# Whole float32 W1out and g in the first half batch, shifts shared with VectorE, and quarters of W1 in alternating order by batch

## The chip, the core and the metric

One of the eight cores of a Trainium2 chip runs the kernel. The metric is device time in microseconds (us) of one execution; lower is better. Engines are named as in the profile: PE (TensorE) with PEld (its weight loads), DVE (VectorE), ACT (ScalarE), POOL (GpSimd), SP (SyncE, which issues most DMAs).

## What is computed

Four batches of 8 heads, 576 tokens and 64 channels go through a Nystrom attention with 32 landmarks; the tokens (2304 x 512) then pass two MLPs with 2048 hidden channels:

```
q_lm, k_lm = q, k averaged over 18 tokens each
A = softmax(q k_lm' / 8); Bm = softmax(q_lm k_lm' / 8); C = softmax(q_lm k' / 8)
Z = 6 Newton steps towards the inverse of Bm
x = A Z C v
h = x @ w_in;  x = (h - tanh(h)) @ w_out                    # first MLP
h = x @ w_in2; out = (h * tanh(softplus(h))) @ w_out2       # second MLP
```

The weights arrive as 64-bit floats and are turned into 32-bit ones on the chip.

## The kernel before

**Order of the work.** The first MLP is a pipeline of 128 slots: four batches of 32, each batch two halves of 288 tokens, each half 16 blocks f of 128 hidden channels. The attention's last product is folded into W1in: P = Z0 times W1in for a batch (`p_gen`, a quarter j of 512 hidden channels at a time, two groups g of heads), and h of a slot is P times the attention weights AT (`h1`, six fp32r matmuls, L511 to L513, on two groups). `vec` then makes g from h on ACT and DVE: a square, a tanh, an exp and another square on ACT; a mask mk, two operations on h, a product and a masked copy on DVE. Two slots later `vec` splits g into a high and a low fp32r half (gg; ACT copies, DVE or POOL subtracts, L99 and L100), and three slots later (LAG = 3) `y1` multiplies it with block f of W1out, split in the same way (w). Each product takes three fp32r matmuls, high by high (L614), low weights by high (L615) and high weights by low g (L618), for four quarters d of the output: 12 a slot. After 16 slots y goes to DRAM (ys). The second MLP follows, in slots of 384 tokens (`h2`, `o2`).

**Weights.** `convert` takes a list of jobs, each a 512 KB load of 64-bit floats into one of four raw buffers (L115). `f32_a` makes the upper part on ACT (L131) and the lower part by a shift, on ACT (L137) or on DVE (L140); `f32_b` merges them on DVE (L144). The list's argument `act_share` says which jobs shift on ACT: all at 1, every second one at 2. A `keep_job` leaves half of a W1in tile (w1) and writes the finished tile to DRAM (w1s, a spill, L171, issued from POOL) for the later batches, which load it back for each `p_gen` (L477). A `split_job` splits a W1out block into w at once (L99, L100). 13 jobs come before the first slot (quarter 0 of W1in, W1out blocks 0 to 8), three more follow, and the rest run beside slots 0 to 11.

**What sets the order.** Up to slot 115 a scheduler orders each engine's instructions by priority and dependencies; from slot 116 they stand as written. Each engine takes its own in order. The helper `E()` gives DVE up to slot 23 and after slot 103, POOL between. The attention of the next batch runs beside slots 5 to 31 of a batch.

## Time and profile before

| | us |
|---|---|
| median of 3 runs (lowest, highest) | 851.7 (851.68, 852.64) |
| the profiled execution's own time | 851.59 |
| its span | 849.8 |
| PE busy | 812.7 (96%) |
| DVE busy | 503.3 (59%) |
| ACT busy | 496.6 (58%) |
| POOL busy | 179.0 (21%) |

The profiled execution takes 1.8 us more than its span, since the span counts from the first instruction to the last. Times below are from the span's start. Busy shares are means over stages with different limits, so they have to be read stage by stage.

### The profile page before, as it was taken

Reading aid. Unit: us, or ns where it says so; the run is one execution under the profiler, and the core shown is the slowest. Engines: PE = TensorE matmul, PEld = TensorE weight load, DVE = VectorE, ACT = ScalarE, POOL = GpSimd, SP = SyncE. Lnnn points to the kernel's source line nnn. Section 1 sums busy time; section 2 is a strip of 40 time slices with the busy share of each in tenths; the row PEclk is TensorE's granted clock in tenths of the full one; section 3 lists DMA queues with packets and bytes.
Section 4 is the critical chain, followed back from the end, with each engine's and each line's share of the span. In section 5 each row is a group of like instructions: output and inputs, shape, how many; then the busy total and the mean of one; then the engine's idle time right before and its main releaser. Section 6 shows DMA issues by size and latency. Waiting matters only on the chain.

```text
span 849.8 us, 15003 instructions
## 1 busy us (share of the span) xinstructions
PE 812.7 (96%) x5656; PEld 706.5 (83%) x5656; DVE 503.3 (59%) x1158; ACT 496.6 (58%) x1234; POOL 179.0 (21%) x210
## 2 busy tenths in 40 slices
PE   4599899999999999999999999999999999999998
PEld 1346689889988899879899999999999999999996
DVE  6878999998789877999973986322111111211111
ACT  5888976788778886799874865333223222222221
POOL 0010003886577666870000000000000000000000
PEclk9557999999999999999999999999999999999999
DMA  9899240430415100360006662022002001000000
GB/s 327 289 338 366 105 136 6 148 136 1 141 51 183 51 30 1 119 215 20 29 2 225 202 195 69 1 66 74 1 1 66 10 1 49 18 1 9 30 1 37
DMA packets 34985, 79.62 MB, mean 94 GB/s; under 512 B 5472, under 2 KB 14176, under 8 KB 34912
## 3 DMA queue, kind: packets, MB, share of 16 engines
q1 hardware_dynamic: 33760, 74.46, 26.0%
q0 software_dynamic: 1152, 4.19, 1.2%
q8 instruction: 44, 0.72, 0.4%
q14 instruction: 29, 0.24, 0.1%
HBM read 65.01 MB, written 13.63 MB: 93 GB/s over the span
## 4 chain that ended last, share of the span: by engine, by line
PE 74%; DVE 12%; ACT 5%; POOL 3%; DMA 2%; issue 2%; SPq 0%; DVEq 0%; ACTq 0%
PE y L642 7%; PE y L638 7%; PE y L637 7%; PE y L614 6%; PE h L537 5%; PE h L536 5%; PE h L535 5%; PE y L618 5%; PE y L615 5%; PE m L211 3%; PE m L537 2%; PE h L511 2%; PE m L536 2%; PE m L535 2%; DVE g L596 2%; PE h L513 2%
## 5 line engine op out<-in xcount | busy, mean ns | idle before, releaser
L585 DVE TENSOR_TENSOR gg<-g,gg 128x384 fp32r<-128x384 f32 x96 | 53.5, 558 | 276.0 <-ACT g L584 276.0
L614 PE MATMUL y<-gg,w 128*128 128x288 f32 x512 | 151.3, 310 | 5.4 <-ACT gg L99 4.1
L615 PE MATMUL y<-gg,w 128*128 128x288 f32 x512 | 143.8, 296 | 0.0
L614 PEld LDWEIGHTS y<-gg,w 128*128 128x128 f32 x512 | 97.0, 189 | 29.4 <-issue 15.3
L618 PE MATMUL y<-gg,w 128*128 128x288 f32 x512 | 109.8, 299 | 1.2 <-DVE gg L100 0.8
L583 ACT ACTIVATE gg<-h 128x384 fp32r<-128x384 f32 x66 | 32.5, 492 | 132.8 <-PE h L537 132.8
L638 PE MATMUL y<-w,gg 128*128 128x512 f32 x256 | 101.2, 395 | 0.0
L637 PE MATMUL y<-w,gg 128*128 128x512 f32 x256 | 100.8, 394 | 0.0
L615 PEld LDWEIGHTS y<-gg,w 128*128 128x128 f32 x512 | 97.5, 190 | 0.0
L100 POOL TENSOR_TENSOR gg<-g,gg 128x288 fp32r<-128x288 f32 x80 | 69.3, 866 | 115.8 <-ACT gg L99 113.8
L642 PE MATMUL y<-w,gg 128*128 128x512 f32 x256 | 88.4, 396 | 0.0
L618 PEld LDWEIGHTS y<-gg,w 128*128 128x128 f32 x512 | 81.7, 189 | 6.3 <-DVE gg L100 2.1
L511 PE MATMUL h<-AT,P 128*128 128x288 f32 x256 | 79.0, 309 | 8.2 <-ACT P L490 5.1
L568 POOL TENSOR_SCALAR mk<-s 128x288 uint8<-128x288 f32 x80 | 77.7, 972 | 10.5 <-ACT s L562 4.3
L513 PE MATMUL h<-AT,P 128*128 128x288 f32 x256 | 77.7, 303 | 0.2 <-DVE P L492 0.2
L512 PE MATMUL h<-AT,P 128*128 128x288 f32 x256 | 77.8, 304 | 0.0
L596 DVE COPY_PREDICATED g<-mk,th 128x288 f32<-128x288 uint8 x128 | 74.3, 580 | 4.6
L99 ACT ACTIVATE gg<-g 128x288 fp32r<-128x288 f32 x128 | 57.1, 446 | 24.3 <-PE y L618 15.4
L578 ACT ACTIVATE q<-q,bias_c 128x288 f32<-128x288 f32 x128 | 69.1, 540 | 2.2
L574 DVE TENSOR_TENSOR g<-h,s 128x288 f32<-128x288 f32 x128 | 56.9, 445 | 19.5 <-ACT th L563 18.9
L583 ACT ACTIVATE gg<-m 128x384 fp32r<-128x384 f32 x30 | 14.8, 492 | 89.2 <-PE m L537 89.2
L562 ACT ACTIVATE s<-h 128x288 f32<-128x288 f32 x128 | 52.6, 411 | 23.9 <-PE h L513 23.8
(162 smaller groups left out, 1856.9 us busy)
## 6 DMA issues: line engine op xcount, KB each, us to landing
w<-w1s SPq DMA_DIRECT2D x24, 512.0 KB, 4.5
raw<-in_w1i_dram SPq DMA_DIRECT2D x16, 512.0 KB, 6.5
raw<-in_w1o_dram SPq DMA_DIRECT2D x16, 512.0 KB, 4.8
raw<-in_w2i_dram SPq DMA_DIRECT2D x16, 512.0 KB, 4.5
raw<-in_w2o_dram SPq DMA_DIRECT2D x16, 512.0 KB, 4.2
ys<-raw SPq DMA_DIRECT2D x16, 288.0 KB, 2.4
out_dram<-raw SPq DMA_DIRECT2D x18, 256.0 KB, 2.2
v<-in_v_dram SPq DMA_DIRECT2D x8, 512.0 KB, 8.5
```

Of the source, the lines that this page charges most:

```text
L100: eng.tensor_tensor(out=L, in0=src, in1=f32(H), op=ALU.subtract)
L511: mm(p, P[:, g, 0, c], AT[:, g, 0, :], start=(g == 0), stop=False)
L512: mm(p, P[:, g, 0, c], AT[:, g, 1, :], start=False, stop=False)
L513: mm(p, P[:, g, 1, c], AT[:, g, 0, :], start=False, stop=(g == NG - 1))
L568: eng.tensor_scalar(out=mk, in0=e, scalar1=FT, scalar2=None, op0=ALU.is_ge)
L596: V.copy_predicated(out=g0, mask=mk0, data=t0)
L614: mm(yps[d], w[:, 0, c], gg[:, 0, :], start=(f == 0), stop=False)
L615: mm(yps[d], w[:, 1, c], gg[:, 0, :], start=False, stop=False)
L618: mm(yps[d], w[:, 0, c], gg[:, 1, :], start=False, stop=(f == NF - 1))
L637: mm(p, gg[:, 0, cs], w[:, 0, :], start=(f == 0), stop=False)
L638: mm(p, gg[:, 0, cs], w[:, 1, :], start=False, stop=False)
L642: mm(p, gg[:, 1, cs], w[:, 0, :], start=False, stop=(f == NF - 1))
```

## The change

In the first half batch (slots 0 to 15, `NW`), y1 multiplies whole float32 g with whole float32 W1out: one matmul for each d (L646 in the changed program), which the chip runs as two instructions. W1out blocks are kept whole by `whole_job` and split by `resplit`, one block a slot in slots 14 to 29. `convert` shifts every second job on DVE. `hidden` lets odd batches take the quarters of W1 in the order 3, 2, 1, 0 (but for the last half batch), so that two quarters of a batch stay in SBUF for the next and only two are loaded back. The prologue converts quarters 0 and 1 and five W1out blocks. Spills of quarters 2 and 3 are written later in the program, at slot 14. The splits of P get a high priority.

```diff
-    NPRE = 9
+    NPRE = 5
+    NW = 16
...
-    wo_p = ctx.enter_context(tc.tile_pool(name="wo", bufs=NF))
+    wo_p = ctx.enter_context(tc.tile_pool(name="wo", bufs=NF + 1))
...
+    def spill(g, j):
+        G.dma_start(out=w1s[g, j], in_=w1t[g, j])
+
+    def whole_job(src, dst, i):
+        def where():
+            W1f[i] = wo_p.tile([128, 2, 512], F32, tag="w", name="w")
+            return W1f[i][:, 0, :]
...
+    def resplit(i):
+        w = wo_p.tile([128, 2, 512], F32R, tag="w", name="w")
+        A.activation(out=w[:, 0, :], in_=W1f[i][:, 0, :], func=ACTF.Copy)
+        yield 1
+        E().tensor_tensor(out=w[:, 1, :], in0=W1f[i][:, 0, :], in1=f32(w[:, 0, :]), op=ALU.subtract)
+        W1o[i] = w
+        yield 1
...
             if a == 1:
-                G.dma_start(out=w1s[g, j], in_=w1t[0, g, j])
+                if j < 2:
+                    spill(g, j)
...
+    def hidden(s):
+        b, hf, p = s // 32, s // 16 % 2, s % 16
+        return 4 * (3 - p // 4) + p % 4 if b % 2 and not (b == B - 1 and hf) else p
...
-        n = 2 * (4 * b + j) + 2
-        if b or j == 3:
-            w1_load(n)
-            w1_load(n + 1)
+        if b and n == 1:
+            w1_load(js[2])
+            w1_load(js[3])
...
-            A.activation(out=P[:, g, 0, :], in_=p, func=ACTF.Copy)
+            with tc.high_priority(60):
+                A.activation(out=P[:, g, 0, :], in_=p, func=ACTF.Copy)
...
-        if 2 <= s < NS + 2:
+        if 2 <= s < NW + 2:
+            sv[s - 2] = sv[s - 2][0]
+        if NW + 2 <= s < NS + 2:
...
-                gg = tp[1].tile([128, 2, C2], F32R, tag="gg", name="gg", bufs=5)
+                gg = tp[1].tile([128, 2, C2], F32R, tag="gg", name="gg", bufs=4)
...
-        w = W1o[f]
-        for d in (2 * half, 2 * half + 1):
+        w = W1o[hidden(s)]
+        for d in (2 * half, 2 * half + 1) if s < NW else ():
+            if f == 0:
+                yps[d] = ps_y.tile([128, 512], F32, tag="y", name="y")[:, 0:HS]
+            mm(yps[d], w[:, 0, 128 * d:128 * d + 128], gg, start=(f == 0), stop=(f == NF - 1))
+        for d in (2 * half, 2 * half + 1) if s >= NW else ():
...
-            return [split_job(src[i], wo_p, "w", dst, i) for i in range(lo, hi)]
+            return [whole_job(src[i], dst, i) for i in range(lo, hi)]
-        jobs = w1i_jobs(0) + wo_jobs(w1o, W1o, 0, NPRE)
-        rest = [(4 * j, n) for j in (1, 2, 3) for n in w1i_jobs(j)]
+        jobs = w1i_jobs(0) + w1i_jobs(1) + wo_jobs(w1o, W1o, 0, NPRE)
+        rest = [(4 * j - 2, n) for j in (2, 3) for n in w1i_jobs(j)]
...
-        cv = vec_only(convert(jobs), rate)
+        cv = vec_only(convert(jobs, 2), rate)
...
+                if i == 14:
+                    for j in (2, 3):
+                        for g in range(NG):
+                            spill(g, j)
+                if NW - 2 <= i < NW - 2 + NF:
+                    streams.append(resplit(i - NW + 2))
```

On PE, the work of one slot's y1. Before (y_695, y_698, y_717 and y_720 are the four quarters d, w_266 a W1out block):

```order
L614 MATMUL y_695<-gg_791,w_266 128x288
L615 MATMUL y_695<-gg_791,w_266 128x288
L614 MATMUL y_698<-gg_791,w_266 128x288
L615 MATMUL y_698<-gg_791,w_266 128x288
L614 MATMUL y_717<-gg_791,w_266 128x288
L615 MATMUL y_717<-gg_791,w_266 128x288
L618 MATMUL y_695<-gg_791,w_266 128x288
L618 MATMUL y_698<-gg_791,w_266 128x288
L614 MATMUL y_720<-gg_791,w_266 128x288
L615 MATMUL y_720<-gg_791,w_266 128x288
L618 MATMUL y_717<-gg_791,w_266 128x288
L618 MATMUL y_720<-gg_791,w_266 128x288
```

and of the change, with the first h matmul behind it:

```order
L646 MATMUL y_687<-g_754,w_505 128x288
L646 MATMUL y_689<-g_754,w_505 128x288
L646 MATMUL y_705<-g_754,w_505 128x288
L646 MATMUL y_707<-g_754,w_505 128x288
L542 MATMUL h_863<-AT_484,P_578 128x288
```

The twelve fp32r matmuls have become four on g itself.

On DVE, one slot in the middle of the first half batch. Before (raw, y: a weight's lower and upper part; w: a W1out block; red: landmark sums of batch 1):

```order
L100 TENSOR_TENSOR gg_950<-g_849,gg_950 128x288
L144 SCALAR_TENSOR_TENSOR y_902<-y_902,raw_753 128x512
L568 TENSOR_SCALAR mk_957<-s_953 128x288
L100 TENSOR_TENSOR w_970<-y_857,w_970 128x512
L574 TENSOR_TENSOR g_955<-h_916,s_953 128x288
L575 TENSOR_TENSOR th_954<-h_916,th_954 128x288
L592 TENSOR_TENSOR g_955<-q_956,g_955 128x288
L250 TENSOR_REDUCE red_837<-k_708 128x64
L596 COPY_PREDICATED g_955<-mk_957,th_954 128x288
```

and of the change:

```order
L141 TENSOR_SCALAR raw_768<-raw_768 128x512
L145 SCALAR_TENSOR_TENSOR w_887<-y_849,raw_733 128x512
L601 TENSOR_SCALAR mk_878<-s_874 128x288
L607 TENSOR_TENSOR g_876<-h_863,s_874 128x288
L608 TENSOR_TENSOR th_875<-h_863,th_875 128x288
L625 TENSOR_TENSOR g_876<-q_877,g_876 128x288
L275 TENSOR_REDUCE red_797<-k_696 128x64
L629 COPY_PREDICATED g_876<-mk_878,th_875 128x288
```

The subtractions for gg and w are gone from the slot, and a shift (L141) has come in.

On POOL, from the last spill on; its first g split is that of slot 22, in slot 24. Before (c: attention of batch 1; xm: its row statistics):

```order
L171 DMA w1s_78<-w1_807 128x1024
L100 TENSOR_TENSOR gg_1828<-g_1745,gg_1828 128x288
L568 TENSOR_SCALAR mk_1835<-s_1831 128x288
L100 TENSOR_TENSOR gg_1875<-g_1792,gg_1875 128x288
L568 TENSOR_SCALAR mk_1882<-s_1878 128x288
L100 TENSOR_TENSOR gg_1915<-g_1833,gg_1915 128x288
L445 TENSOR_TENSOR c_1087<-c_1087,xm_1893 128x288
L568 TENSOR_SCALAR mk_1922<-s_1918 128x288
L445 TENSOR_TENSOR c_1087<-c_1087,xm_1934 128x288
L100 TENSOR_TENSOR gg_1956<-g_1880,gg_1956 128x288
```

and of the change:

```order
L165 DMA w1s_78<-w1_722 128x1024
L101 TENSOR_TENSOR gg_1648<-g_1559,gg_1648 128x288
L601 TENSOR_SCALAR mk_1655<-s_1651 128x288
L183 TENSOR_TENSOR w_1637<-w_887,w_1637 128x512
L101 TENSOR_TENSOR gg_1698<-g_1609,gg_1698 128x288
L601 TENSOR_SCALAR mk_1705<-s_1701 128x288
L183 TENSOR_TENSOR w_1680<-w_921,w_1680 128x512
L183 TENSOR_TENSOR w_1733<-w_956,w_1733 128x512
L101 TENSOR_TENSOR gg_1741<-g_1653,gg_1741 128x288
L601 TENSOR_SCALAR mk_1748<-s_1744 128x288
L183 TENSOR_TENSOR w_1777<-w_999,w_1777 128x512
L470 TENSOR_TENSOR c_972<-c_972,xm_1717 128x288
```

Six W1out subtractions (L183, two more come further on) now stand between the g splits and masks, ahead of batch 1's attention. In both programs the spills follow each other at the front of POOL's queue with nothing between them.

## Rows read from the trace of the kernel before

**Rows 1.** Stages: window, length, busy PE, PEld, DVE, ACT, POOL, clock, DMA, GB/s.

```profile
0.00:45.00 45.00, 24.63 (x285) 11.53 (x286) 33.45 (x85) 32.98 (x73) 2.00 (x8) 0.70 0.89 309
45.00:83.00 38.00, 36.42 (x169) 21.14 (x170) 33.09 (x79) 30.59 (x73) 3.30 (x6) 0.68 0.96 353
83.00:114.00 31.00, 25.75 (x185) 20.75 (x184) 29.95 (x77) 27.56 (x75) 0.00 (x0) 1.00 0.26 96
114.00:139.00 25.00, 25.00 (x336) 22.50 (x335) 23.68 (x71) 18.96 (x53) 0.00 (x0) 1.00 0.36 120
139.00:163.00 24.00, 23.54 (x199) 20.11 (x198) 21.24 (x47) 18.75 (x50) 19.12 (x22) 1.00 0.15 50
```

**Rows 2.** The chain that ended last: start us, us, what; from 84.21 DVE throughout.

```profile
50.76 8.44 DMA raw<-in_w1i_dram
...
84.21 0.69 DVE w L100
...
106.93 0.38 DVE th L575
```

**Rows 3.** PE's timeline (start us, us): last h of slots 0, 8, 16, 24.

```profile
45.14 0.44 PE L513 MATMUL h<-AT,P 128*128 128x288 f32 x1
...
83.40 0.30 PE L513 MATMUL h<-AT,P 128*128 128x288 f32 x1
...
113.67 0.30 PE L512 MATMUL h<-AT,P 128*128 128x288 f32 x1
113.81 0.30 PE L513 MATMUL h<-AT,P 128*128 128x288 f32 x1
...
139.01 0.30 PE L513 MATMUL h<-AT,P 128*128 128x288 f32 x1
```

**Rows 4.** PE's timeline: a burst of fp32 matmuls and the next fp32r one.

```profile
333.56 0.72 PE L211 MATMUL m<-q,kb 64*32 64x288 f32 x16
334.20 0.40 PE L614 MATMUL y<-gg,w 128*128 128x288 f32 x1
```

**Rows 5.** Groups by line, 0 to 114 us: count, busy us, mean ns, idle before.

```profile
L144 DVE SCALAR_TENSOR_TENSOR y<-y,raw 128x512 uint32<-128x512 uint32 x16 | 10.9, 682 | 1.7 <-ACT raw L137 1.4
L100 DVE TENSOR_TENSOR w<-y,w 128x512 fp32r<-128x512 f32 x16 | 10.9, 682 | 0.8 <-ACT w L99 0.8
L100 DVE TENSOR_TENSOR gg<-g,gg 128x288 fp32r<-128x288 f32 x14 | 6.2, 443 | 0.6 <-ACT gg L99 0.6
...
L137 ACT ACTIVATE raw<-raw 128x512 uint32<-128x512 uint16 x32 | 21.5, 670 | 0.0
```

**Rows 6.** The shift on DVE, in the second MLP (min/median/max ns).

```profile
L140 DVE TENSOR_SCALAR raw<-raw x13: 419/421/426, 458.4 to 533.6; 128x512 uint32<-128x512 uint32 x13
```

**Rows 7.** The page's DMA issues: W1 tiles loaded back.

```profile
w<-w1s SPq DMA_DIRECT2D x24, 512.0 KB, 4.5
```

**Rows 8.** Timelines of PE and ACT: P of quarter 0, and its first copy.

```profile
34.63 1.96 PE L211 MATMUL m<-w,z 64*32 64x512 f32 x16 [0.93 <-ACT z L415]
...
39.70 0.57 ACT L490 ACTIVATE P<-m 128x512 fp32r<-128x512 f32 x1
```

**Rows 9.** Timelines: POOL's g splits of slots 22 and 29; PE's use of the latter.

```profile
139.08 0.81 POOL L100 TENSOR_TENSOR gg<-g,gg 128x288 fp32r<-128x288 f32 x1 [63.54 <-ACT gg L99]
...
160.60 0.89 POOL L100 TENSOR_TENSOR gg<-g,gg 128x288 fp32r<-128x288 f32 x1
...
161.99 0.43 PE L618 MATMUL y<-gg,w 128*128 128x288 f32 x2
```

**Rows 10.** POOL's groups by line, 139 to 163 us.

```profile
L568 POOL TENSOR_SCALAR mk<-s 128x288 uint8<-128x288 f32 x8 | 7.7, 962 | 0.7
L100 POOL TENSOR_TENSOR gg<-g,gg 128x288 fp32r<-128x288 f32 x8 | 6.9, 866 | 66.7 <-ACT gg L99 66.6
L100 POOL TENSOR_TENSOR AT<-c,AT 128x288 fp32r<-128x288 f32 x2 | 1.6, 808 | 0.3 <-ACT AT L99 0.3
L457 POOL TENSOR_TENSOR c<-c,xm 128x288 f32<-128x288 f32 x2 | 1.5, 760 | 0.2
```

More of the change, by code (lines that the diff above doesn't have):

```diff
@@ L161, in split_job, with done @@
         return src, done, None
+    def spill(g, j):
[4 more added lines that the diff above has]
+            return W1f[i][:, 0, :]
+        def done(y):
+            dst[i] = W1f[i]
+        return src, done, where
+    W1f = {}
+    def resplit(i):
[5 more added lines that the diff above has]
+        yield 1
     def keep_job(src, g, j, a):
@@ L165, in where @@
             if a == 0:
-                w1t[0, g, j] = w1_p.tile([128, 2, 512], F32, tag="w1", name="w1")
-            return w1t[0, g, j][:, a, :]
+                w1t[g, j] = w1_p.tile([128, 2, 512], F32, tag="w1", name="w1")
+            return w1t[g, j][:, a, :]
         def done(y):
             if a == 1:
-                G.dma_start(out=w1s[g, j], in_=w1t[0, g, j])
+                if j < 2:
+                    spill(g, j)
                 if g:
@@ L470, with w1_load, p_gen @@
     done = set()
-    def w1_load(n):
-        b, j, g = n // 8, n // 2 % 4, n % 2
-        if b < B:
-            t = w1_p.tile([128, 2, 512], F32, tag="w1", name="w1")
-            w1t[b, g, j] = t
-            nc.sync.dma_start(out=t, in_=w1s[g, j])
-    def p_gen(b, j):
-        ws = [w1t.pop((b, g, j)) for g in range(NG)]
+    def hidden(s):
+        b, hf, p = s // 32, s // 16 % 2, s % 16
+        return 4 * (3 - p // 4) + p % 4 if b % 2 and not (b == B - 1 and hf) else p
+    def w1_load(j):
+        for g in range(NG):
+            w1t[g, j] = w1_p.tile([128, 2, 512], F32, tag="w1", name="w1")
+            nc.sync.dma_start(out=w1t[g, j], in_=w1s[g, j])
+    def p_gen(b, n):
+        js = [hidden(32 * b + 4 * i) // 4 for i in range(4)]
+        j = js[n]
         P = Pt[b, j] = P_p.tile([128, NG, 2, 512], F32R, tag="P", name="P")
         pp = [ps_m.tile([128, 512], F32, tag="m", name="m") for g in range(NG)]
-        blocks(pp, Z0, lambda ps, g, a: ws[g][ps, a, :])
-        n = 2 * (4 * b + j) + 2
-        if b or j == 3:
-            w1_load(n)
-            w1_load(n + 1)
+        blocks(pp, Z0, lambda ps, g, a: w1t[g, j][ps, a, :])
+        if b and n == 1:
+            w1_load(js[2])
+            w1_load(js[3])
         yield 1
         for g, p in enumerate(pp):
-            A.activation(out=P[:, g, 0, :], in_=p, func=ACTF.Copy)
+            with tc.high_priority(60):
+                A.activation(out=P[:, g, 0, :], in_=p, func=ACTF.Copy)
             yield 0
-            V.tensor_tensor(out=P[:, g, 1, :], in0=p, in1=f32(P[:, g, 0, :]), op=ALU.subtract)
+            with tc.high_priority(60):
+                V.tensor_tensor(out=P[:, g, 1, :], in0=p, in1=f32(P[:, g, 0, :]), op=ALU.subtract)
             yield 0
@@ L504, in h1 @@
     def h1(s):
-        b, hf, f = s // 32, s // 16 % 2, s % 16
+        b, hf, f = s // 32, s // 16 % 2, hidden(s)
         AT, P = ATt[b, hf], Pt[b, f // 4]
@@ L615, in y1 @@
             mm(yps[d], w[:, 1, c], gg[:, 0, :], start=False, stop=False)
-        for d in (2 * half, 2 * half + 1):
+        for d in (2 * half, 2 * half + 1) if s >= NW else ():
             c = slice(128 * d, 128 * d + 128)
@@ L779 @@
                     del live[k]
-            if "pre" not in live and ready and nc_ >= 4 + NPRE - 1:
+            if "pre" not in live and not Pt and nc_ >= 8 + NPRE - 1:
                 pg = p_gen(0, ready.pop(0))
@@ L783 @@
                 gens.append(pg)
-            if (nc_ < 4 + NPRE or (nc_ < PREP and "pre" not in live)):
+            if (nc_ < 8 + NPRE or (nc_ < PREP and "pre" not in live)):
                 part(cv)
@@ L813, in bg @@
                 mix.append(cv)
+                if i == 14:
+                    for j in (2, 3):
+                        for g in range(NG):
+                            spill(g, j)
+                if NW - 2 <= i < NW - 2 + NF:
+                    streams.append(resplit(i - NW + 2))
                 while ready and i:
```

## The prediction

> **What bounds the kernel now.** I read the stages first, then the slots' marks, the chain, and single rows. A slot is one of the 128 steps of the first MLP; slot s is marked by its last h matmul (L513). In the table of stages [rows 1] the reader is to see three regimes. Up to 83 us TensorE, VectorE and ScalarE all have gaps or a lowered clock (granted 0.70 and 0.68 of full speed on the mean, so a large part of the time at the 1.2 GHz level instead of 2.4), and the DMA engines are 0.89 and 0.96 busy. From 83 to 114 us DMA is down to 0.26 and VectorE is busy 29.95 of 31 us. From 114 us on TensorE is busy without a break (25.00 of 25, then 23.54 of 24). The chain says the same [rows 2]: a W1in load (50.76 us, 8.44 long) in the first regime, an unbroken run of VectorE work from 84.21 to 106.93 us in the second, TensorE after it. So what can be gained lies before slot 16; what is lost later, in a stretch that TensorE fills, is lost for good. The marks [rows 3]: h of slot 0 at 45.14 us, slot 8 at 83.40, slot 16 at 113.81, slot 24 at 139.01.
>
> **The change, part by part.**
>
> *fp32 matmuls.* In slots 3 to 18 a slot's 12 fp32r matmuls on y become 4 fp32 ones of two instructions each (8). fp32r: 0.13 us from start to start (113.67 and 113.81 [rows 3]). For fp32 the nearest row is a burst of 8 fp32 matmuls that run side by side, so two steps of 288 columns: 333.56 to 334.20, 0.64 us, the switch to fp32r included [rows 4]. Two instructions cost at least four fp32r passes, 0.52, and at most 0.64. I take 0.26 per instruction and 0.14 per slot for switching: 8 x 0.26 + 0.14 = 2.2 instead of 12 x 0.13 = 1.6, so +0.6 us a slot, 10 us of TensorE work in all (bounds +0.5 and +1.0 a slot).
>
> *g not split.* Away go 16 subtractions of 0.443 us on VectorE [rows 5] and as many copies on ScalarE. That also shortens the way from g to y1.
>
> *W1out whole, split later.* 16 copies on ScalarE and 16 subtractions of 0.682 us on VectorE [rows 5] leave the start and come back one per slot in slots 14 to 29: by the order 10 subtractions stand on VectorE and 6 on POOL, since the helper picks POOL from slot 24.
>
> *Shifts shared.* 16 of 32 shifts leave ScalarE (0.670 us each [rows 5], 10.7 us) and become VectorE's at 0.421 us [rows 6] (6.7 us).
>
> *Quarters.* 12 of the 24 reloads of W1 go (512 KB each [rows 7]); four of them stood in SP's queue ahead of the last two W1out loads. At 353 GB/s [rows 1] four are 5.9 us of DMA time, but at the end of the loading, where VectorE already sets the pace: I give nothing for it (bounds 0 and -2). If VectorE weren't the cover, the last W1out loads would come that much earlier.
>
> *Spills.* The program issues those of quarters 2 and 3 at slot 14, but POOL's queue holds nothing before them, and each waits only for its data; so they go out when they did before. Cost and gain zero; a rival below says otherwise. *Buffers:* gg with 4 instead of 5 is reused after its slot's matmuls of one slot earlier; TensorE runs in order, so nothing waits: zero. The 17th W1out tile lets the first split in; without it the splits would wait for y1.
>
> **The sum, stage by stage**, with instructions counted in the order:
>
> 1. *To slot 0.* The first P copy stood ready but behind conversions on ScalarE until 39.70 us, though its matmuls had ended at 36.59 [rows 8]. Nine of the ScalarE splits and seven shifts are gone there, and VectorE has 9 splits and 2 merges of 0.682 us less [rows 5] and 7 shifts of 0.421 more, -4.6 us. So h of slot 0 moves from 45.14 to about 39.6: -5.5 (bounds -2.5, where loads bind, to -7).
> 2. *Slots 0 to 8, 38.3 us before.* VectorE: 7 g splits and 2 W1out splits less, 7 shifts and 2 merges more: -3.1 - 1.4 + 2.9 + 1.4, nothing. DMA: the same bytes at 0.96 [rows 1]. TensorE: six slots of fp32, +3.6, partly in gaps. I take 41.3 us (bounds 38 and 44): slot 8 at 80.9.
> 3. *Slots 8 to 16, 30.4 us before.* VectorE loses 8 x 0.443 + 5 x 0.682 and gains 2 x 0.682 + 2 x 0.421: -4.7 from 30, 25.2. TensorE: eight slots at 6 x 0.13 + 2.2 = 3.0, 24, and batch 1's small attention matmuls of about 3: 27.3 us, now the bound. Slot 16 at 108.2.
> 4. *Slots 16 to 24, 25.2 us before.* TensorE +1.3 (12 fp32 matmuls are left). VectorE had 23.68 of 25 [rows 1]; 8 W1out splits more, one g split and one reduction less, +3.7: level with TensorE. 26.5 us; slot 24 at 134.7, 4.3 earlier than before.
> 5. *Slots 24 to 29: POOL.* From its first g split (139.08) to the end of that for slot 29 (161.49) POOL took 22.4 us, and TensorE uses it at 161.99 [rows 9]: 0.5 us of slack. POOL now does in the same order 8 g splits of 0.866, 7 masks of 0.962, 2 AT splits of 0.808, 4 of attention's operations at 0.76 [rows 10] and 6 W1out splits. A 128x512 subtraction doesn't occur on POOL before: at least 0.866 (if width cost nothing), at most 1.54 (by width). I take 1.45, near the upper end, since rows of one width tell no fixed part. 6.9 + 6.7 + 1.6 + 3.0 + 8.7 = 27.0 us, 4.6 more than before; I set the 0.5 of slack against the gaps between POOL's instructions, which the sum leaves out. TensorE waits for all of it: +4.6 (bounds +0.6 and +6). Behind the waiting low half stand all later h and y matmuls, so the loss isn't made up.
>
> -4.3 + 4.6 = +0.3 on the profiled execution's 851.6, 851.9; the median is 0.1 above that execution: **852.0 us**.
>
> The Trainium skill (GPSIMD Engine Reference, 2.1 Instruction dispatch) puts an operation of two inputs on GpSimd at no less than about 2.5 cycles an element at 1.2 GHz. That agrees with the row (0.60 us of 0.866 for 288 elements), and with the rest of the row as a fixed part 512 elements would take an estimated 1.33 us; six of these give 0.7 us less, a sum of 851.3.
>
> **The rivals.**
>
> *POOL keeps up* (faster). If the W1out split on POOL is near its lower bound, stage 5 costs 0.6, and the time is 851.6 - 4.3 + 0.6 + 0.1 = 848; a clock that rises before 65 us, since TensorE is denser, would bring stage 2 to its lower bound, 3 more: 845. For: POOL was idle 4.9 of 24 us [rows 1]. Against: 6 operations need 5.2 us even at the lower bound. 0.20.
>
> *The spills are late after all* (faster). If they did wait for slot 14, 2.1 MB would leave the saturated stretch, 5.9 us at 353 GB/s: 846. The order speaks against it. 0.10.
>
> *Loads bind the start* (slower). If the first 14 raw loads land when they did, ScalarE's and VectorE's relief is spent waiting: slot 0 comes 2.5 earlier, not 5.5, and the rest stands: 855. For: DMA at 0.89 from the beginning [rows 1]. Against: loads were issued as conversions freed buffers. It decides where merged work waits for landings in 30 to 45 us. 0.18.
>
> *TensorE becomes the bound too soon* (slower). At 0.32 an instruction, or with weight loads that show, the fp32 stretch costs 128 x 0.06 = 7.7 more; it decides once a slot's TensorE time passes VectorE's 25.2 / 8 = 3.15 us, so above 0.28 an instruction: most of it is lost, 858. 0.14.
>
> **How the numbers follow.** A measurement tells about 0.2% (1.7 us) from no change. The forecast, no measurable difference, has 0.38. Faster: 0.20 + 0.10, and 0.01 from the forecast's edge. Slower: 0.18 + 0.14. The range takes in 846 and 857: the forecast's own bounds, the faster cases, the loads' case and the smaller half of the last. The forecast's own range is 849 to 854.
>
> **What would show it.** After: slot 0 near 39.6 us, slot 8 near 81, 16 near 108, 24 near 135; VectorE no longer full in slots 8 to 16, with TensorE at 3.0 to 3.4 us a slot; POOL busy without gaps for some 27 us from slot 24 and y's low-half matmuls waiting for it; spills issued as each quarter is merged. It is wrong if slot 24 isn't 2 to 6 us earlier, if POOL's subtraction is under 1.2 us, or if TensorE never waits for POOL in slots 25 to 31.

## The result: 0.9% slower, and the profile after

The changed kernel takes 859.75 us (median of 4 runs, 858.82 to 862.81) beside 851.69 us (4 runs of the kernel before on the same chip): a ratio of 1.0089 with a 95% interval of 1.0071 to 1.0108 (the quotient of the two medians alone is 1.0095). The profiled execution took 858.82 us, with a span of 857.0 us instead of 849.8.

The same stages as in [rows 1], now of the changed kernel (window, length, busy PE, PEld, DVE, ACT, POOL, clock, DMA, GB/s):

```profile
0.00:45.00 45.00, 24.61 (x295) 11.27 (x295) 30.40 (x84) 23.50 (x56) 3.19 (x10) 0.71 0.91 311
45.00:83.00 38.00, 30.88 (x141) 16.88 (x136) 31.61 (x77) 27.39 (x62) 2.13 (x4) 0.90 0.94 325
83.00:114.00 31.00, 29.64 (x193) 21.23 (x197) 28.88 (x78) 24.07 (x66) 0.00 (x0) 1.00 0.18 59
114.00:139.00 25.00, 25.00 (x309) 21.87 (x299) 24.89 (x70) 21.38 (x56) 1.99 (x2) 1.00 0.36 120
139.00:163.00 24.00, 19.59 (x151) 15.91 (x150) 17.65 (x36) 16.03 (x42) 21.83 (x23) 1.00 0.13 45
```

Up to 83 us ScalarE is relieved (23.50 us instead of 32.98 in the first stage), yet nothing ends much sooner. From 83 to 114 us TensorE is the busy engine now, not VectorE. From 139 to 163 us the picture turns over: POOL is busy 21.83 of 24 us, while TensorE falls from 23.54 to 19.59.

The last h matmul of slots 0, 8, 16, 24, 29 and 33 in PE's timeline of the changed kernel (start us, us), to be read against [rows 3]:

```profile
43.29 0.61 PE L544 MATMUL h<-AT,P 128*128 128x288 f32 x1
...
83.81 0.29 PE L544 MATMUL h<-AT,P 128*128 128x288 f32 x1
...
111.13 0.29 PE L544 MATMUL h<-AT,P 128*128 128x288 f32 x1
...
136.87 0.30 PE L544 MATMUL h<-AT,P 128*128 128x288 f32 x1
...
154.61 0.30 PE L544 MATMUL h<-AT,P 128*128 128x288 f32 x1
...
172.24 0.30 PE L544 MATMUL h<-AT,P 128*128 128x288 f32 x1
```

The two missing marks of the kernel before, for slots 29 and 33:

```profile
153.56 0.29 PE L513 MATMUL h<-AT,P 128*128 128x288 f32 x1
...
166.94 0.30 PE L513 MATMUL h<-AT,P 128*128 128x288 f32 x1
```

| stretch | before | forecast | after |
|---|---|---|---|
| to slot 0 | 45.1 | 39.6 | 43.3 |
| slots 0 to 8 | 38.3 | 41.3 | 40.5 |
| slots 8 to 16 | 30.4 | 27.3 | 27.3 |
| slots 16 to 24 | 25.2 | 26.5 | 25.7 |
| slots 24 to 33 | 27.9 | +4.6 (by slot 29) | 35.4 (+7.4) |
| slot 33 to the end of the span | 682.8 | 0 | 684.8 (+2.0) |

So 2.1 us are won by slot 24, 7.4 are lost in the next nine slots, and 2.0 after that. Three stretches came out near the forecast; the first and the last two did not.

The chain of work that ended last, up to 84 us and from 102 us (start us, us, what):

```profile
29.55 8.62 DMA raw<-in_w1o_dram
...
69.52 11.24 DMA raw<-in_w1o_dram
```

```profile
102.86 2.43 PE y L646 x10
```

Loads at first, then float32 matmuls. The profile counts instructions, two for each of the 64 float32 matmuls (L646 has 128), so ten in 2.43 us are 0.243 us each; the forecast had 0.26. What TensorE waited for from 137 to 175 us (total us, times, longest):

```profile
PE y L655 <- POOL gg L101: 2.6, 4, 1.3
PE m L236 <- DVE P L523: 1.5, 1, 1.5
PE h L542 <- DVE th L608: 1.3, 1, 1.3
PE y L651 <- ACT gg L100: 0.6, 1, 0.6
```

Only 2.6 of these 6.0 us are put down to POOL; the end of VectorE's work is named for 2.8. That was the first sign that POOL's own time is not the whole story.

### The profile page after: what moved, and what is told of

Read it like the earlier page. It is cut to its first block, busy times and chain, and to the rows that moved or that the text cites. A ratio compares the mean times of both kernels' runs of the same rounds, so it can differ in the third digit from the quotient of the medians.

```text
span 857.0 us, 14800 instructions
## 1 busy us (share of the span) xinstructions
PE 811.1 (95%) x5592; PEld 700.4 (82%) x5592; DVE 499.9 (58%) x1152; ACT 484.4 (57%) x1202; POOL 189.0 (22%) x216
## 4 chain that ended last, share of the span: by engine, by line
PE 73%; DVE 10%; ACT 6%; DMA 5%; POOL 4%; issue 2%; SPq 0%; DVEq 0%; ACTq 0%; POOLq 0%
PE y L679 7%; PE y L675 7%; PE y L674 7%; PE h L568 5%; PE h L567 5%; PE h L566 5%; PE y L651 4%; PE y L652 4%; PE y L655 4%; PE y L646 3%; PE h L542 3%; PE m L568 2%; PE m L567 2%; PE m L566 2%; DMA raw<-in_w1o_dram 2%; PE h L544 2%
## 5 line engine op out<-in xcount | busy, mean ns | idle before, releaser
L651 PE MATMUL y<-gg,w 128*128 128x288 f32 x448 | 131.1, 307 | 2.7 <-ACT gg L100 1.3
L652 PE MATMUL y<-gg,w 128*128 128x288 f32 x448 | 125.2, 295 | 0.0
L651 PEld LDWEIGHTS y<-gg,w 128*128 128x128 f32 x448 | 84.1, 188 | 22.4 <-issue 12.6
L655 PE MATMUL y<-gg,w 128*128 128x288 f32 x448 | 96.4, 296 | 2.8 <-POOL gg L101 2.6
L652 PEld LDWEIGHTS y<-gg,w 128*128 128x128 f32 x448 | 84.4, 188 | 0.1
L655 PEld LDWEIGHTS y<-gg,w 128*128 128x128 f32 x448 | 71.4, 188 | 4.3 <-POOL gg L101 4.2
L542 PEld LDWEIGHTS h<-AT,P 128*128 128x128 f32 x256 | 49.0, 192 | 20.9 <-DVE th L608 11.2
L625 DVE TENSOR_TENSOR g<-q,g 128x288 f32<-128x288 f32 x128 | 63.6, 497 | 3.1 <-ACT q L611 2.0
```

The lines of the kernel that those rows point to most:

```text
L542: mm(p, P[:, g, 0, c], AT[:, g, 0, :], start=(g == 0), stop=False)
L651: mm(yps[d], w[:, 0, c], gg[:, 0, :], start=(f == 0), stop=False)
L652: mm(yps[d], w[:, 1, c], gg[:, 0, :], start=False, stop=False)
L655: mm(yps[d], w[:, 0, c], gg[:, 1, :], start=False, stop=(f == NF - 1))
```

## The experiments

Each run was timed beside the kernel before on the same chip. Ratios are to it; the changed kernel stands at 1.0089. The table has, for six slots, how much later (+) or earlier (-) in us the slot's mark comes than in the kernel before, from one profiled execution each. Such a difference can be off by 2 to 3 us in the start: e16, e22 and e23 run the same instructions up to slot 8 and stand there at -4.4, -6.4 and -6.2. The kernel before and e18 run the same instructions up to 80 us, but slot 5 comes at 72.82 us in the one and at 69.74 in the other. The stretch from 65 to 73 us of the two, in the order of [rows 1]:

```profile
65.00:73.00 8.00, 8.00 (x31) 3.95 (x31) 6.15 (x18) 5.38 (x13) 0.53 (x1) 0.53 1.06 388
```

```profile
65.00:73.00 8.00, 8.00 (x55) 5.61 (x54) 8.00 (x22) 7.65 (x20) 0.53 (x1) 1.00 1.05 377
```

TensorE is busy throughout in both, at a granted clock of 0.53 in the kernel before and 1.00 in e18. The medians don't hang on it: of the 17 runs of the kernel before beside e1, those with a mean clock under 0.985 have a median of 852.25 us and the others 852.48. So the verdicts rest on the ratios, and the marks show where a loss lies when several runs agree.

| run | slot 0 | 8 | 16 | 24 | 33 | 104 | ratio, 95% interval |
|---|---|---|---|---|---|---|---|
| changed kernel | -1.9 | +0.4 | -2.7 | -2.1 | +5.3 | +6.8 | 1.0089 (1.0071 to 1.0108) |
| e1 | -2.3 | +1.4 | -1.7 | -1.1 | +4.4 | +6.3 | 1.0079 (1.006 to 1.0097) |
| e2 | -2.8 | +1.9 | +1.0 | +0.6 | +1.1 | +2.7 | 1.0012 (0.9999 to 1.0024) |
| e4 | -0.7 | +5.1 | +6.4 | +6.4 | +6.4 | +8.2 | 1.0087 (1.0074 to 1.01) |
| e7 | -4.1 | -0.6 | -3.7 | -3.2 | +4.3 | +7.2 | 1.0076 (1.0061 to 1.0092) |
| e13 | -2.2 | +1.8 | +0.2 | +0.7 | +6.7 | +8.3 | 1.0077 (1.006 to 1.0093) |
| e8 | -4.4 | -0.7 | +0.3 | +7.1 | +7.1 | +9.3 | 1.0106 (1.0081 to 1.0131) |
| e5 | -1.9 | +1.4 | -1.6 | -1.1 | +6.4 | +8.0 | 1.0081 (1.0061 to 1.0102) |
| e6 | +0.7 | +2.3 | +5.3 | +5.3 | +5.3 | +5.3 | 1.0042 (1.0028 to 1.0055) |
| e18 | -0.0 | -3.0 | -1.6 | -1.6 | -1.6 | +0.6 | 1.003 (1.002 to 1.0039) |
| e3 | -1.9 | -3.9 | -4.8 | -3.7 | +3.3 | +5.0 | 1.0052 (1.0033 to 1.007) |
| e20 | -4.1 | +3.1 | -0.5 | +1.2 | +2.7 | +5.4 | 1.0054 (1.0039 to 1.007) |
| **e16** | -3.3 | -4.4 | -3.8 | -4.2 | -3.7 | -2.0 | **0.9956 (0.9944 to 0.9968)** |
| e22 | -5.4 | -6.4 | -1.5 | +1.2 | +3.5 | +5.1 | 1.0059 (1.004 to 1.0078) |
| e23 | -5.1 | -6.2 | -4.0 | -4.4 | -2.4 | -0.8 | 0.998 (0.9964 to 0.9995) |

### The late splits: e1, e13 and e2

The subtraction of `resplit` on VectorE alone (e1):

```diff
-        E().tensor_tensor(out=w[:, 1, :], in0=W1f[i][:, 0, :], ...
+        V.tensor_tensor(out=w[:, 1, :], in0=W1f[i][:, 0, :], ...
```

> Edit: the late W1out split's subtraction is always VectorE's, so none is on POOL. Theory (POOL is the bound from slot 24 to 33, where the changed kernel loses 7.4 us against the kernel before: -2.1 at slot 24, +5.3 at slot 33): the marks up to slot 24 stay within 0.3 us, slot 33 comes 5 to 7 us earlier than in the changed kernel, and the time falls from 859.75 to 853 to 855. Rival (the loss comes from batch 1's attention being late, or VectorE takes POOL's place with 6 subtractions of 0.68 us more): slot 33 moves by less than 2 us, the time stays above 858.

The time was 858.92 us, as the rival had it. Up to slot 30 POOL's share showed (-0.3 against the kernel before, where the changed kernel has +1.7), but 4.7 us went by slot 33 all the same. The rows of e1's timelines there, of ACT, DVE and PE (start us, us, ..., [idle before <- what ended it]):

```profile
154.28 0.44 ACT L473 ACTIVATE c<-c 128x288 f32<-128x288 f32 x1 [2.08 <-POOL c L470]
...
156.19 1.29 DVE L523 TENSOR_TENSOR P<-m,P 128x512 fp32r<-128x512 f32 x2 [1.55 <-ACT P L520]
...
158.10 0.91 DVE L183 TENSOR_TENSOR w<-w 128x512 fp32r<-128x512 f32 x1
...
162.21 0.40 PE L542 MATMUL h<-AT,P 128*128 128x288 f32 x1 [2.96 <-DVE th L608]
```

VectorE stood waiting for ScalarE before P's subtraction, and the late split took 0.91 us (1.13 at 151.58) instead of 0.68. The P work has a raised priority in the changed kernel, so the next run took that away for batches 1 to 3.

```diff
-            with tc.high_priority(60):
+            with tc.high_priority(0 if b else 60):
```

> Edit: the late splits on VectorE as in the run e1, and the raised priority of the P copies and subtractions only for batch 0. In the run e1 TensorE kept pace to slot 30 (-0.3 against the kernel before) and then lost 4 to 5.5 us in slots 31 to 33: VectorE stood 1.55 us at a P subtraction whose ScalarE copy was queued behind a wait for POOL. Theory A (the raised P work of batch 1, put ahead in the in-order queues, is what blocks): slot 33 at +0.5 to +1.5 against the kernel before instead of +4.4, and the steps of +0.6 us in slots 38, 70 and 102 go, so 853.5 to 855. Theory B (what blocks is the sum of work in slots 28 to 32: late splits, P and batch 1's attention at once on ScalarE and VectorE): slot 33 stays at +3.5 or more, and only the later steps go: 857 to 858.5.

The time was 859.82 us, with slot 33 at +6.7: theory B for the place, but the later steps stay too. So P's priority isn't the cause. The splits were then moved out of the stretch instead, to slots 8 to 23 (e2; with `E()` that is VectorE):

```diff
-                if NW - 2 <= i < NW - 2 + NF:
-                    streams.append(resplit(i - NW + 2))
+                if 8 <= i < 8 + NF:
+                    streams.append(resplit(i - 8))
```

> Edit: the 16 W1out splits stand one per slot in slots 8 to 23 instead of 14 to 29, all on VectorE. Theory (only POOL's share costs; in slots 8 to 16 TensorE is the bound with 3.4 us a slot and VectorE has room): slot 16 later by at most 1 us than in the changed kernel (111.1), slot 24 equal or earlier (136.9), slot 33 5 to 8 us earlier, time 852 to 855. Rival (VectorE becomes the bound in slots 8 to 16, 6 subtractions of 0.68 us and as many copies on ScalarE more): slot 16 at 114 or later, and the time stays at 856 or more.

The time was 854.02 us, within the theory's range. Slots 24 to 33 now take 0.5 us more than before the change, not 7.4; slot 16 came 3.7 us later than in the changed kernel (the rival's value for that mark, not for the time), with VectorE busy 30.64 of the 31 us from 83 to 114. The loss of slots 24 to 33 belongs to the splits' place beside POOL's work, batch 1's attention and its first P, on whichever engine they run.

### POOL and VectorE: e8, e22 and e23

If VectorE is full in slots 8 to 16 and POOL is idle until slot 24, the early splits could go to POOL (e8, which also has the order of e7 and the priority of e13):

```diff
-        E().tensor_tensor(out=w[:, 1, :], in0=W1f[i][:, 0, :], ...
+        G.tensor_tensor(out=w[:, 1, :], in0=W1f[i][:, 0, :], ...
```

> Edit: late splits in slots 8 to 23 with the subtraction on POOL (idle there), quarter 1's loads behind the first W1out loads, P priority raised only for batch 0. In the run e2 the same splits on VectorE cost 3.7 us in slots 12 to 16. Theory (POOL has 3.1 us a slot and needs 1.3; VectorE is relieved by 0.68 a slot): slot 8 at -0.6, slot 16 at -3 to -4, slot 24 at -3 to -4.5 against the kernel before, no steps in slots 29 to 33 and 38, 70, 102: 847 to 850, under the kernel before. Rival (VectorE's operations beside a busy POOL take longer, as the 0.46 us product took 1.29 at 157 us in the changed kernel): slot 16 at -1 or later, and 851 to 854.

The time was 861.42 us, the slowest of all: the rival in kind, but 7 us beyond its range, though POOL was busy for only 10.89 of 31 us from 83 to 114. Most of it was lost from slot 16 to 24 (+0.3 to +7.1). Two splits on POOL, and what VectorE did beside them (e8's timelines; L402 and L406 work on two numbers a partition, L608 reads h from PSUM):

```profile
118.43 1.29 POOL L183 TENSOR_TENSOR w<-w 128x512 fp32r<-128x512 f32 x1 [0.74 <-DVE g L607]
120.46 1.28 POOL L183 TENSOR_TENSOR w<-w 128x512 fp32r<-128x512 f32 x1 [0.74 <-ACT w L181]
```

```profile
118.35 0.14 DVE L379 TENSOR_TENSOR n<-n 128x2 f32<-128x2 f32 x1
118.42 0.44 DVE L608 TENSOR_TENSOR th<-h,th 128x288 f32<-128x288 f32 x1
118.78 0.96 DVE L402 TENSOR_SCALAR n<-n 128x2 f32<-128x2 f32 x1
...
120.52 1.24 DVE L406 TENSOR_TENSOR n<-n,rc 128x2 f32<-128x2 f32 x1
```

Two 128x2 operations, which take about 0.15 us elsewhere (L379 here: 0.14), end at 119.74 and 121.76 us, just as POOL's splits do at 119.72 and 121.74. The one on h ran beside POOL in its normal 0.44 us. In these two places VectorE did not run slower, it waited until POOL was done. Since ScalarE's copies also waited for POOL in e8, two runs separate the two: e16 (below) with POOL work that nothing waits for (e22's trace names no instruction that waited for it), once reading and once, but for one element, only writing.

```diff
+        G.tensor_tensor(out=scr[:, 0:448], in0=W1f[i][:, 0, 0:448],
+                        in1=f32(w[:, 0, 0:448]), op=ALU.subtract)      # e22
```

```diff
+        G.tensor_copy(out=scr[:, 448:449], in_=f32(w[:, 0, 0:1]))     # e23
+        G.memset(scr, 0.0)
+        G.memset(scr, 0.0)
+        G.memset(scr, 0.0)
```

> Edit: run e16 (849.4 us, late splits on VectorE in slots 8 to 23) and, beside each of the 16 late splits, one subtraction of 128x448 on POOL into a scratch tile that nobody reads. Theory (VectorE's operations that read two operands from SBUF, and its scalar operations between SBUF tiles, stand still while POOL's two-input operation runs, as a 128x2 product did for 1.24 us in the run e8): the subtractions take about 1.1 us each on POOL; L625, L629 and L601 on VectorE get longer in slots 8 to 24, those that read h from PSUM do not; VectorE is nearly full in slots 8 to 16, so slot 24 comes 4 to 10 us later than in e16 and the time is 853 to 859. Rival (POOL's dummy work costs nothing, the loss of the run e8 came from ScalarE's copies waiting for POOL's split to free a tile): 849 to 850.5.

> Edit: the same as the run e22, but POOL only writes: a copy of one element per partition, to keep its place in time, and three memsets of 128x449 beside each of the 16 late splits, about 1 us of POOL work. If it is POOL's reading that stops VectorE, VectorE's durations stay as in e16 and the time is 849 to 851. If any POOL work stops VectorE (or costs elsewhere), the time is as in e22, 853 to 859.

The time was 858.02 us with the reading work and 850.27 with the writing, both as their theories had them. From slot 8 to 24, e22 loses 7.6 us, e16 0.2 and e23 1.8; at slot 24 e23 stands level with e16 (-4.4 and -4.2). The groups by line and form from 90 to 135 us (xcount, busy us, mean ns): the masked copy (of e16 alone), the product of h from PSUM, the product q g (two operands in SBUF) and the mask, of e16, e22 and e23, and last in e22's POOL's reading work (from 80 us on):

```profile
L629 DVE COPY_PREDICATED g<-mk,th 128x288 f32<-128x288 uint8 x14 | 6.8, 487 | 0.0
L607 DVE TENSOR_TENSOR g<-h,s 128x288 f32<-128x288 f32 x15 | 6.8, 453 | 0.4 <-ACT th L596 0.4
L625 DVE TENSOR_TENSOR g<-q,g 128x288 f32<-128x288 f32 x14 | 6.3, 452 | 0.0
...
L601 DVE TENSOR_SCALAR mk<-s 128x288 uint8<-128x288 f32 x15 | 4.6, 304 | 0.0
```

```profile
L627 DVE TENSOR_TENSOR g<-q,g 128x288 f32<-128x288 f32 x12 | 7.7, 643 | 0.0
...
L609 DVE TENSOR_TENSOR g<-h,s 128x288 f32<-128x288 f32 x13 | 5.9, 450 | 0.0
...
L603 DVE TENSOR_SCALAR mk<-s 128x288 uint8<-128x288 f32 x13 | 5.8, 447 | 0.0
...
L185 POOL TENSOR_TENSOR scr<-w 128x448 f32<-128x448 f32 x14 | 17.2, 1226 | 52.3 <-ACT w L182 52.3
```

```profile
L612 DVE TENSOR_TENSOR g<-h,s 128x288 f32<-128x288 f32 x15 | 6.7, 446 | 0.4 <-ACT th L601 0.4
L630 DVE TENSOR_TENSOR g<-q,g 128x288 f32<-128x288 f32 x14 | 6.2, 446 | 0.0
...
L606 DVE TENSOR_SCALAR mk<-s 128x288 uint8<-128x288 f32 x14 | 4.6, 328 | 0.0
```

POOL's reads lengthen the product from 452 to 643 ns, the mask from 304 to 447 and the masked copy from 487 to 539, and leave the product on h at 450. POOL's writes, which take more of its time than forecast (it is busy for 30.45 us from 83 to 139, with the reads for 18.36), leave all of these alone but the mask (328). The Trainium skill says of the product's kind (SBUF — State Buffer, Who interferes with whom): a VectorE instruction with two inputs in SBUF contends with a GpSimd instruction that reads SBUF, not with one that only writes it. Here the runs agree.

### The start: e7, e5, e3 and e6

In the changed kernel the first P copy stood behind conversions whose loads came late (ACT's timeline):

```profile
38.26 0.66 ACT L132 ACTIVATE y<-raw 128x512 f32<-128x512 f32 x1 [2.12 <-DMA raw<-in_w1o_dram]
...
39.36 1.07 ACT L520 ACTIVATE P<-m 128x512 fp32r<-128x512 f32 x2
```

Four spills went out before 40 us (at 17.37, 21.99, 28.48 and 31.16 us on POOL) instead of two, since quarter 1 is loaded ahead of W1out. e7 puts it behind:

```diff
-        jobs = w1i_jobs(0) + w1i_jobs(1) + wo_jobs(w1o, W1o, 0, NPRE)
+        jobs = w1i_jobs(0) + wo_jobs(w1o, W1o, 0, NPRE) + w1i_jobs(1)
```

> Edit: the loads of quarter 1 of W1in stand behind the first 5 of W1out instead of ahead of them, so that its two spills (1 MB) go out later. Theory (the start is bound by DMA: four spills of 0.5 MB instead of two before 40 us, at about 330 GB/s 3 us more): the first P copy at 36.5 to 38 instead of 39.4 us, slot 0 at 40.5 to 42 instead of 43.3; slot 8 as before (83.8), since the same bytes go through the queues by then, and the time within 1.5 us of 859.75. Rival (the start is bound by something else, by the way of the conversions through 4 raw buffers): slot 0 stays within 0.5 us of 43.3.

The first P copy comes at 37.23 us and the third spill at 38.24 (e7's timelines), slot 0 2.2 us earlier than in the changed kernel. The six runs with this order (e7, e8, e20, e16, e22, e23) have slot 0 at -3.3 or earlier, the five that share the changed kernel's loads and shifts (it, e1, e2, e5, e13) at -2.8 or later. The time is 859.45 us, which is not clear of noise by itself: as expected, only 1 us is left at slot 8. Whether the two spills or the order of the loads did it was not tried apart. e5 takes batch 1's v loads out of the way of W1out's:

```diff
                     for g in range(NG):
                         attn_load(b + 1, g)
-                    for g in range(NG):
-                        v_load(b + 1, g)
...
+                if i == (3 if b else 11):
+                    for g in range(NG):
+                        v_load(b + 1, g)
```

> Edit: batch 1's v (4 loads, 1.15 MB) is loaded in slot 11 instead of 3; it stood on SP ahead of the last 5 W1out loads, one of which took 11.24 us to land. Theory (slots 0 to 8 are bound by DMA, so 1.15 MB at about 330 GB/s are 3.5 us): slots 4 to 8 come 1 to 3.5 us earlier than in the changed kernel (65.4, 83.8); slot 16 less, since TensorE is the bound there, 0.5 to 2 us; the loss from slot 24 on stays, so 857.5 to 859.5. Rival (conversions on ScalarE and VectorE set slots 0 to 8): slot 8 within 0.5 us of 83.8, 859.75.

The time was 859.8 us, with slots 4 and 8 no earlier (1.5 and 1.0 us later, which is within the scatter): the rival's time. 1.15 MB less ahead of a load that took 11.24 us to land bought nothing, so the conversions themselves are the next suspect. e3 has their shifts back on ScalarE (`convert(jobs)` instead of `convert(jobs, 2)`):

> Edit: the changed kernel with all shifts on ScalarE again. In the kernel before the shared shifts alone cost 5.3 us up to slot 16 (run e6). Theory A (there because VectorE was full in slots 8 to 16; in the changed kernel 14 of the shared shifts lie before 85 us, where DMA sets the pace, and TensorE sets slots 8 to 16): all marks within 0.7 us of the changed kernel, 858.5 to 860.5. Theory B (VectorE's shifts delay the merges, and so the freeing of raw buffers and the loads, in both kernels): slots 4 to 16 come 1.5 to 4 us earlier, 855.5 to 858.

The time was 857.11 us, with slot 4 2.0 and slot 8 4.3 us earlier than in the changed kernel, as theory B had it in size; slot 0 is where it was. The other runs agree: slots 0 to 8 take 36.3 to 37.3 us in e3, e16, e22 and e23, with these shifts on ScalarE, and 40.5 to 43.0 in the changed kernel, e1, e2, e5, e7, e8 and e13. By what path is less clear. TensorE's waits for VectorE's th (L608) from 43 to 84 us fall from 4.1 us to 1.2, so part of it is VectorE's own work for the slots; the last seven W1out loads were issued over 17.85 us instead of 20.25, but only after slot 4. The shifts alone, in the kernel before (e6):

> Edit: the kernel before with only the shared shifts: 16 of 32 shifts on VectorE (0.42 us each). Theory (in the kernel before VectorE sets slots 8 to 16, so each of its 16 x 0.42 = 6.7 us that falls where it is full costs): slot 0 1 to 2 us earlier or equal, slot 16 3 to 7 us later than 113.8, the time 855 to 859. That would explain why the changed kernel without its float32 W1out (run e4) loses 6.4 us up to slot 16. Rival (it is the order of the loads and spills that costs there): slot 16 within 1 us, 851 to 853.

The time was 856.4 us, with +5.3 at slot 16 and nothing after, as the theory had it (but for slot 0, 0.7 us later). VectorE has no room for them there.

### The whole float32 itself, the quarters, and a mixture: e4, e18 and e20

e4 is the changed kernel without the whole float32 (W1out is split at its conversion, g as before):

```diff
-    NW = 16
+    NW = 0
...
-            return [whole_job(src[i], dst, i) for i in range(lo, hi)]
+            return [split_job(src[i], wo_p, "w", dst, i) for i in range(lo, hi)]
```

> Edit: the changed kernel with W1out and g split in the first half batch as before (no float32 matmuls, no late splits); shared shifts, quarters, order of the loads and priorities stay. Theory (the loss is that of the whole float32 W1out: TensorE's 0.6 us a slot and POOL's payback): no loss in slots 24 to 33, but VectorE is full again in slots 8 to 16, with 7 us of shifts more, so slot 16 near 114 to 116, time 852 to 855. Rival (the other parts of the change, the order of the loads and the quarters, cost by themselves): the time stays at 858 or more.

The time was 859.77 us, which is the rival's, and equal to the changed kernel by another way: +6.4 at slot 16 and then level up to slot 33, as the theory had it for that stretch. So beside shared shifts the float32 W1out wins 9.1 us up to slot 16 (+6.4 to -2.7), and its late splits give 8.0 back up to slot 33 (-2.7 to +5.3). What it wins with the shifts on ScalarE was not tried. e18 is the kernel before with `hidden` and the halved reloads alone:

> Edit: the kernel before with only the quarters of W1 in alternating order and 12 of the 24 reloads gone. Every version with the quarters so far loses about 0.4 to 0.8 us at each of slots 38, 70 and 102 against the kernel before, about 1 us in all. Theory (that step comes from the quarters: the order of P, attention and masks on VectorE around the fourth P of a batch): up to slot 34 within 0.5 us of the kernel before, or up to 2 earlier at slot 16 where four reloads no longer stand ahead of the last W1out loads, then +0.8 to +1.2 by slot 104; 851 to 853. Rival (the step comes from P's priority or the smaller buffer count of the changed kernel): no steps, and 850 to 852.

The time was 855.45 us, slower by 0.3%. The profiled execution is the fastest of the twelve (span 851.0), so its marks show the steps and not the whole price: 3.0 us earlier at slot 8, which is the scatter shown above, then +2.2 from slot 34 to 104, in steps of 1.1 us at slots 38 and 39 and again at 70 and 71. The steps are the quarters', and the time was longer than either side had it. e20 keeps only W1out blocks 8 to 15 whole and splits them in slots 16 to 23, with the order of e7 and all shifts on ScalarE:

```diff
+            return [whole_job(src[i], dst, i) if i >= 8
+                    else split_job(src[i], wo_p, "w", dst, i) for i in range(lo, hi)]
...
+                if 16 <= i < 24:
+                    streams.append(resplit(i - 8))
```

> Edit: only tiles 8 to 15 of W1out stay whole in float32 (used in slots 8 to 15, where VectorE was full in the kernel before); tiles 0 to 7 and g of slots 0 to 7 are split as before; the 8 late splits stand in slots 16 to 23 on VectorE; quarter 1's loads behind the first W1out loads; all shifts on ScalarE. Theory (each stretch gets its work where it has room; no split is left for slots 24 to 31, where POOL and VectorE block each other): slot 8 at -1 to +1 against the kernel before, slot 16 at -2 to -4, slot 24 and 33 at -1.5 to -3.5, the later steps +1: 848.5 to 851. Rival (splits in slots 0 to 8 delay the loads' buffers as in the run e4, +5 at slot 8): 854 or more.

The time was 857.8 us, as the rival had it, with +3.1 at slot 8. That the splits do it by delaying the loads isn't shown: the last seven W1out loads begin at 66.72 us, in e16 at 69.24, and come later than there only from the third on (75.06 and 73.26); also, the granted clock from 66 to 82 us was under 0.8, in e16 1.00.

### What they add up to: e16

e16 is the changed kernel with three of these edits: the late splits in slots 8 to 23 (e2), quarter 1's loads behind W1out's (e7) and the shifts on ScalarE (e3).

> Edit: three edits together: late splits in slots 8 to 23 on VectorE (run e2, -5.3 us up to slot 33), quarter 1's loads behind the first W1out loads (run e7, -1 us at slot 8), all shifts on ScalarE. If the three add up: slot 8 at -0.5 to -1.5 against the kernel before, slot 16 within 1 us of it, slot 33 at -0.5 to -1.5, and with the 1 us of the later steps 851 to 853, level with the kernel before. Rival (the runs' gains lie on the same stretch, where DMA sets slots 0 to 8): slot 8 at +1 or more as in the run e2, 853.5 to 855.

The time was 849.36 us (5 runs, 848.3 to 849.49), 0.44% faster than the kernel before and better than the forecast for it. By the ratios the single edits are worth 0.77%, 0.13% (not clear of noise) and 0.37%, together 1.27%; the three at once 1.33%. They nearly add up. Two of e16's stages:

```profile
45.00:83.00 38.00, 33.20 (x146) 18.00 (x138) 31.81 (x74) 29.68 (x69) 2.66 (x5) 0.94 0.97 344
...
139.00:163.00 24.00, 22.85 (x200) 18.62 (x197) 21.81 (x52) 18.39 (x51) 18.78 (x22) 1.00 0.26 91
```

From 45 to 83 us DMA moves 344 GB/s instead of 325, and from 139 to 163 us TensorE is busy 22.85 of 24 us beside POOL's usual work.

## Why the prediction was wrong

The forecast was 852.0 us (846 to 857); the changed kernel takes 859.75. Worked out by its own steps on the profiled executions, the miss is 6.9 us in the span: +3.7 in step 1, -0.8 in step 2, 0 in step 3, -0.8 in step 4, +2.8 in step 5, and +2.0 where it had put nothing. The rest is the median, which lies 0.9 us above the profiled execution.

- **"To slot 0: -5.5" failed.** It measured -1.9, outside its own bound of -2.5. The figure was taken between its bounds, not added up. The step counted the work that leaves ScalarE and VectorE and took the loads to follow. The relieved engines waited for loads instead: the 13 loads before slot 0 became 8 of W1in and 5 of W1out, with two more spills among them. And since each engine takes its instructions in order, the attention's short operations on the way to P stood behind conversions that waited for a load: v behind a merge whose W1out load landed at 32.02 us, z behind a conversion of the load that landed at 35.20 (DVE's, ACT's and PE's timelines of the changed kernel):

```profile
33.33 0.69 DVE L145 SCALAR_TENSOR_TENSOR w<-y,raw 128x512 uint32<-128x512 uint32 x1 [1.72 <-ACT raw L138]
33.94 0.28 DVE L432 SCALAR_TENSOR_TENSOR v<-yv,m 128x128 f32<-128x128 f32 x1
```

```profile
35.28 0.69 ACT L132 ACTIVATE y<-raw 128x512 f32<-128x512 f32 x1 [1.65 <-DMA raw<-in_w1o_dram]
35.87 0.27 ACT L440 ACTIVATE z<-m 128x128 f32<-128x128 f32 x1
```

```profile
36.19 1.96 PE L236 MATMUL m<-w,z 64*32 64x512 f32 x16 [1.22 <-ACT z L440]
```

  Before the change v and z (DVE's and ACT's timelines) came more than a microsecond earlier:

```profile
32.66 0.29 DVE L407 SCALAR_TENSOR_TENSOR v<-yv,m 128x128 f32<-128x128 f32 x1 [0.17 <-PE m L218]
```

```profile
34.32 0.25 ACT L415 ACTIVATE z<-m 128x128 f32<-128x128 f32 x1
```

  P's matmuls ended at 36.59 us then; now they end at 38.15, and the P copy stands behind one more conversion until 39.36. In e7 they end at 37.14 and the copy follows at 37.23: its 2.2 of the 3.7 us are the spills' and loads' order. With the shifts on ScalarE as well, e22 and e23 reach slot 0 at 39.7 and 40.1 us, but e16, the same program up to there, at 41.8; their granted clock from 20 to 45 us was 1.00, 1.00 and 0.50. So the last 1.5 us stay open. The rival "loads bind the start" named the place and had 0.18; its price (855) was too low, since the others missed too.
- **Steps 2 to 4 held in number, step 2 by luck.** Forecast 41.3, 27.3 and 26.5; measured 40.5, 27.3 and 25.7. Step 2 put its 3 us on TensorE's float32 matmuls and nothing on VectorE; e3, with the same matmuls and without the shared shifts, needs 36.3. So the time came from the shifts, which the step had put at nothing. Also, the 38.3 us from which it started are of an execution with the low clock shown above (e18: 35.3). Step 4's +1.3 for TensorE doesn't follow from its own +0.6 a slot (three float32 slots are +1.8), and +0.5 was measured. In steps 3 and 4 the mechanism held: TensorE set the pace (29.64 of 31 us, then 25.00 of 25), and VectorE was level with it in slots 16 to 24 (24.89 of 25 us). The float32 matmul was mis-sized a little: 0.243 us an instruction and not 0.26.
- **"Slots 24 to 29: POOL, +4.6" failed, in size and extent.** The groups of POOL in the changed kernel, 134 to 175 us:

```profile
L101 POOL TENSOR_TENSOR gg<-g,gg 128x288 fp32r<-128x288 f32 x10 | 9.6, 958 | 70.8 <-ACT gg L100 70.7
...
L183 POOL TENSOR_TENSOR w<-w 128x512 fp32r<-128x512 f32 x6 | 7.9, 1317 | 1.3 <-ACT w L181 1.0
```

  The six splits took 1.32 us each, less than the 1.45 of the sum; the estimate by the Trainium skill (GPSIMD Engine Reference, 2.1 Instruction dispatch) of 1.33 was the better one. What the step left out is the other engine: it costed POOL's queue alone and let VectorE run beside it. A split on POOL and VectorE's product q g beside it, which takes 0.45 us when POOL is idle (e16's rows):

```profile
156.90 1.29 POOL L183 TENSOR_TENSOR w<-w 128x512 fp32r<-128x512 f32 x1 [0.29 <-ACT w L181]
```

```profile
157.20 1.29 DVE L625 TENSOR_TENSOR g<-q,g 128x288 f32<-128x288 f32 x1 [0.39 <-ACT q L611]
```

  From 139 to 175 us the product takes 672 ns on the mean, before the change 462, and the masked copy 717 instead of 630:

```profile
L625 DVE TENSOR_TENSOR g<-q,g 128x288 f32<-128x288 f32 x10 | 6.7, 672 | 1.6 <-ACT q L611 1.6
L629 DVE COPY_PREDICATED g<-mk,th 128x288 f32<-128x288 uint8 x9 | 6.5, 717 | 0.3
```

  That such operations of VectorE wait while POOL reads is shown by e8, e22 and e23. Against their times beside an idle POOL (452 and 487 ns in e16) an estimate from these rows is 4.3 us of waiting in the two groups, and before the change 1.8. How much of the 7.4 us it makes in this stretch is not shown, since batch 1's attention and P add their waits there, and e1 lost nearly as much with the splits on VectorE; e2 shows only that all but 0.5 us goes when the splits leave the stretch. And the step ended at slot 29 (+3.2 by then), while the backlog ran into slots 30 to 33, where P and the attention of batch 1 stand (+4.2 more). "The loss isn't made up" held: slot 40 is at +5.9, slot 96 at +6.4.
- **"Quarters: I give nothing" failed.** The forecast weighed only transfers. e18, which has this part alone, is 0.3% slower than the kernel before, with steps of 1.1 us at slots 38 and 70; the changed kernel has steps at 38, 70 and 102, 1.5 us of the 2.0 after slot 33. The new order moves the P work of odd batches beside the attention; that this makes the steps was not traced.
- **"Shifts shared" was sized right and valued wrongly.** Each takes 0.42 us on VectorE, as forecast; step 2 then set them off against g splits that were gone. Undone, they give 4.3 us at slot 8 (e3); added alone to the kernel before, they cost 5.3 us at slot 16 (e6).
- **The other rivals.** POOL did not keep up, TensorE did not become the bound too soon (0.243 us, under the 0.28 from which it was to decide), and the spills were not late: the last went out at 68.2 us. None of the three things that were to prove the forecast wrong occurred (slot 24 was 2.1 us earlier, POOL's subtraction over 1.2 us, TensorE did wait for POOL); they tested steps 4 and 5 in kind, not in size.
